# Zero matmuls between the first attention pairs: their number, their place and the PSUM bank they write

## The chip, the cores and the metric

The kernel runs on one core of a Trainium2 chip. The metric is the device time of one execution in microseconds (us), as the median of several runs. The engines are PE (matmul; PEld is its weight load), DVE (vector), ACT (scalar), POOL (gpsimd, which here mostly starts transfers) and SP (transfers). Each engine takes its own instructions in the order in which the program gives them, and waits on semaphores for the others.

## The reference

There are 8 batches, 8 heads, 576 positions and head size 64. Each head computes two attentions and adds them: one over q, k and v averaged over groups of 4 positions (144 positions, result repeated 4 times), one over a band of 7 neighbouring positions. The result goes through a gated feed-forward layer with 512 inputs and 1536 hidden units.

```
q_d = q.reshape(B, H, S/4, 4, D).mean(axis=3)        # k_d, v_d alike
out_up = repeat(softmax(scale * q_d @ k_d.T) @ v_d, 4, axis=2)
mask = abs(i - j) < 4
out_local = softmax(where(mask, scale * q @ k.T, -1e9)) @ v
x = (out_up + out_local).transpose(0, 2, 1, 3).reshape(B * S, 512)
out = (maximum(x @ w_gate, 0) * (x @ w_val)) @ w_out
```

## The kernel before

The 64 heads are worked in 32 pairs. The feed-forward layer runs over 9 chunks of 512 tokens. All orders are written out by hand: the string FRONT (L18) lists the steps of the fill, in which pairs 0 to 7 and the first chunk are brought up; ORDER (L109) is the steady state, which interleaves attention for later pairs with matmuls of the chunk that is ready; TAIL (L74) is the end. A step is a token, kind/pair/arguments, and a program loop issues the tokens one by one, so a token's place fixes its place on every engine that it uses.

The steps of the fill that matter here, for a pair p:

- loadq, loadk, loadv start the transfers of q, k and v on POOL's queue (L304, L334); only pair 0's q comes by SP's queue (L304). wg and wv fetch a quarter each of the two weight matrices (L799).
- tr/p/i/bank (emit_flip, L364) transposes q and k: 8 matmuls with 120 columns each, against an identity with pooling columns. ev copies the result from PSUM, on ACT where its token has an A, on DVE where it has a V (L378); its argument says which third, and whether the full or the pooled part.
- vd (L408) pools v with 6 matmuls into bank 6, columns 0 to 255, and vc (L417, ACT) copies that out.
- s1 (L427, L438) computes both score matrices into banks 0 to 3. ed (L462) and ex (L448) take the exponentials on ACT, and ma (L454, DVE) applies the band mask.
- sd (L475) and su (L487) multiply by v. sd writes bank 6, su banks 4 and 5. rd, td, ru, tu (L499, L504, L512, L518, all DVE) divide by the denominators and write the tile xo.
- xp (L622, L624) transposes and adds the two results on PE; xe (L634) copies them to xT, the input of the feed-forward layer.
- hv and hg (L639) are the first matmuls of the feed-forward layer.

The step warm (emit_warm, L810 to L818) issues matmuls whose two operands are the tile zero_sb, which holds zeros, and whose result nobody reads. The call before FRONT issues 12 of 128x512 into bank 7. In FRONT, warm/2 stands twice: behind pair 0's transposes and pooled v, and ahead of pair 1's pooled v (vd/1). These write 248 columns of bank 6 (264 to 511), so each is ordered against other users of that bank. In the profile all of them have line L812.

The eight PSUM banks are one tile, ps. A matmul that writes a bank waits for earlier readers of that bank where the program finds an overlap.

Of the kernel before, what the change touches and what calls it, by code (L numbers as in the profile page):

```python
# [16 lines left out]

FRONT = """  # L18
pads loadk/0 loadv/0 loadq/1 loadk/1 loadv/1 loadq/2 cast tr/0/2/4 loadk/2 ev/0/20V/4 tr/0/1/3
tr/0/0/2 ev/0/21V/4 ev/0/10A/3 vd/0/6 loadv/2 ev/0/11A/3 ev/0/01A/2 ev/0/00A/2 loadq/3 warm/2  # L20
tr/1/0/7 vc/0/6 s1/0/2 ev/1/00A/7 loadk/3 tr/1/2/1 ed/0/2 tr/1/1/0 ev/1/20V/1 ev/1/11A/0 loadv/3
sd/0/6 ev/1/21V/1 ev/1/10A/0 rd/0/6 ex/0/0/2 td/0/6 wg/0 warm/2 vd/1/6 ev/1/01A/7 ma/0/0
ex/0/1/2 s1/1/0 wv/0 ma/0/1 ed/1/0 ones/4 su/0/4 ex/1/1/0 ru/0/4 loadq/4 ex/1/0/0 tu/0/0/4
tr/2/1/2 tr/2/2/3 tu/0/1/4 ev/2/11A/2 tr/2/0/0 ev/2/10A/2 loadk/4 ev/2/21V/3 xp/0/0/4 ev/2/20V/3
ev/2/01A/0 xp/0/1/5 ev/2/00A/0 ma/1/0 loadv/4 vc/1/6 s1/2/0 ma/1/1 xe/0/0A/4 xe/0/1V/5 sd/1/6
ex/2/1/0 ones/5 su/1/4 rd/1/6 td/1/6 ed/2/0 ru/1/4 vd/2/6 loadq/5 tu/1/1/4 ex/2/0/0 tr/3/1/2
tu/1/0/4 tr/3/2/3 loadk/5 vc/2/6 tr/3/0/0 ev/3/20V/3 ev/3/10A/2 xp/1/1/5 sd/2/6 ev/3/21V/3
loadv/5 ev/3/01A/0 xe/1/1V/5 xp/1/0/4 ev/3/00A/0 ma/2/0 ev/3/11A/2 ma/2/1 xe/1/0A/4 s1/3/0 wg/1
rd/2/6 su/2/4 td/2/6 ed/3/0 ru/2/4 ex/3/0/0 tu/2/1/4 hv/0/0/7 wv/1 hv/0/1/7 tu/2/0/4 ex/3/1/0
vd/3/6 ma/3/0 ones/6 xp/2/1/5 vc/3/6 xp/2/0/4 ma/3/1 sd/3/6 xe/2/1V/5 xe/2/0A/4 loadq/6 tr/4/0/0  # L30
rd/3/6 su/3/4 td/3/6 tr/4/1/2 loadk/6 ru/3/4 hv/1/0/1 ev/4/11A/2 tu/3/0/4 hg/0/0/6 ev/4/10A/2
hg/0/1/6 tu/3/1/4 loadv/6 tr/4/2/3 ev/4/01A/0 ev/4/00A/0 xp/3/1/5 ev/4/21V/3 ev/4/20V/3 xp/3/0/4
wg/2 hv/0/2/7 xe/3/1V/5 xe/3/0A/4 hg/1/0/0 s1/4/2 wv/2 hv/0/3/7 ex/4/0/2 hv/1/1/1 loadq/7
# [136 lines left out]
def kernel(  # L170
# [50 lines left out]
    def ring(n, shape, dtype, name):  # L221
        return [keep.tile(shape, dtype, name=f"{name}{i}") for i in range(n)]
# [14 lines left out]
    ed = ring(2, [72, 2, 2 * SD + 64], FP16, "ed_")  # L237
    vd = ring(3, [72, 2, 192], FP16, "vd_")
# [11 lines left out]
    ps = psum.tile([128, 8, 512], FP32, name="ps")  # L250
# [45 lines left out]
    def emit_load_q1(hp, i):  # L296

        b, off = head_off(hp)
        src, dst, hh = (q, k)[i // 2], qk16[hp % NL][:, i // 2, :], i % 2
        if hp < NTP:  # L300
            if hh:
                return
            first = hp == 0 and src is q
            (nc.sync if first else nc.gpsimd).dma_start(  # L304
                (q32 if first else dst).rearrange("p (n d) -> p n d", d=64),
                _dap(src, off, [[D, 96], [NQ * D, 2 * NB], [1, D]]),
            )
            return
        nc.gpsimd.dma_start(  # L309
            dst.rearrange("p (j h d) -> p j h d", h=2, d=64)[:, :, hh, :],  # L310
            _dap(src, off + hh * S * D, [[D, 96], [NQ * D, NB], [1, D]]),
        )
# [182 lines left out]
    rd = ring(2, [72, 2, 2], FP32, "rd_")  # L495
    ru = ring(2, [96, 2, NB], FP32, "ru_")
# [310 lines left out]
            _dap(moe_w_out, 384 * i * D_MODEL, [[D_MODEL, 128], [128 * D_MODEL, 3], [1, D_MODEL]]),  # L807
        )

    def emit_warm(n, wide=False):  # L810
        for _ in range(n):
            nc.tensor.matmul(  # L812
                out=ps[:, 7, :] if wide else ps[:, 6, 264:512],
                lhsT=zero_sb[:, 0:128],
                rhs=zero_sb[:, 128 : 640 if wide else 376],
                start=True,
                stop=True,
            )  # L818
# [114 lines left out]
    def emit_tail_step(kind, arg, at):  # L933
        c, j = (int(at[0]), int(at[1])) if len(at) == 2 else (int(at or 0), 0)
        i = int(arg[0]) if arg else 0
        if kind in ("hg", "hv"):
            w = int(kind == "hv")
            bank = 4 + i if w else 2 * (j % 2) + i
            emit_h_mm(c, j + NK * i, w, range(4), ps[:, bank, :])
        elif kind == "relu":  # L940
            emit_relu(2 * j + i, ps[:, 2 * (j % 2) + i, :])
        elif kind == "gate":
            emit_gate(c, j + NK * i, 2 * j + i, ps[:, 4 + i, :])
        elif kind in ("gateg", "gateb"):
            nc.vector.scalar_tensor_tensor(
                out=gT[c % 2][:, j + NK * i, :],
                in0=block(c, j, 0).t[i],
                scalar=0.0,
                in1=ps[:, 4 + i, :] if kind == "gateg" else block(c, j, 1).t[i],
                op0=ALU.max,  # L950
                op1=ALU.mult,
            )
        elif kind == "xs":
            emit_xs(c, i)
        elif kind == "wg":
            emit_ws(0, i, 0, 768, nc.vector)
        elif kind == "wv":
            emit_ws(1, i, 192 * int(arg[1]), 192 * int(arg[1]) + 192, nc.gpsimd)
        elif kind in ("qg", "qv"):
            block(c, j, int(kind == "qv")).q(i)  # L960
        elif kind in ("keepg", "keepv"):
            block(c, j, int(kind == "keepv")).keep(i - 1)
        elif kind in ("tg", "tv"):
            block(c, j, int(kind == "tv")).out(arg)
        elif kind == "part":
            lo, hi = ((0, 3), (3, 5), (5, 6))[int(arg[1])]
            unit(c, j).sums(lo, hi, (i,))
        else:
            UNIT_STEPS[kind](unit(c, j), i)

    def emit_step(kind, arg, u, c):

        banks = (u, 1 - u)
        i = int(arg[-1]) if arg and arg[-1].isdigit() else 0
        if kind in H_STEPS:
            pp, jj = banks[i % 2], 6 * u + i
            if kind == "relu":
                emit_relu(i, pair(pp)[:, 0, :])
            elif kind == "gate":
                emit_gate(c, jj, i, pair(pp)[:, 1, :])  # L980
            else:
                w = int(kind == "hv")
                emit_h_mm(c, jj, w, range(4), pair(pp)[:, w, :])
        elif kind in UNIT_STEPS:
            UNIT_STEPS[kind](unit(c - 1, u), i)
        elif kind == "next":
            w = unit(c - 1, 1) if u == 0 else unit(c, 0)
            w.sums(0, NK if u == 0 else 5, (i,))
        else:
            PAIR_STEPS[kind](4 * c + 2 * u + LEAD + "ab".index(arg[0]), arg[1:])  # L990
# [45 lines left out]
    def emit_periods(c0, c1):  # L1036
        for base in range(c0, c1 + 2):
            for tok in ORDER.split():
                c = base + {">": 1, "<": -1}.get(tok[-1], 0)
                kind, arg, u = tok.rstrip("<>").split("/")  # L1040
                if c == c1 - 1 and base > c:
                    continue
                if c0 <= c < c1 or c == c0 - 1 and f"{kind}/{arg}/{u}" in LATE:
                    emit_step(kind, arg, int(u), c)

    def emit_front(tok):
        kind, *a = tok.split("/")
        if "@" in tok:
            emit_step(kind, a[0], *map(int, a[1].split("@")))
        else:  # L1050
            FRONT_STEPS[kind](*[int(x) if x.isdigit() else x for x in a])

    FRONT_STEPS = {
        "pads": emit_pads,
        "cast": lambda: nc.scalar.copy(out=qk16[0][:, 0, :], in_=q32),
        "warm": emit_warm,
        "loadq": lambda p: emit_load_q1(p, 0),
        "loadk": lambda p: emit_load_q1(p, 2),
# [37 lines left out]
    with tc.manual_schedule(engines={ET.PE, ET.DVE, ET.Activation, ET.SP, ET.Pool}):  # L1096
        nc.scalar.dma_start(cst_sb[:, 960:1080], cst_dr[:, 960:1080])
        emit_load_q1(0, 0)
        nc.sync.dma_start(cst_sb[:, 0:960], cst_dr[:, 0:960])
        nc.sync.dma_start(cst_sb[:, 1080:1368], cst_dr[:, 1080:1368])  # L1100
        emit_warm(12, True)
        for tok in FRONT.split():
            emit_front(tok)
        emit_periods(PS // 4, (NP - LEAD) // 4)
        for tok in TAIL.split():
            kind, arg, *at = tok.split("/")
            if at:
                emit_tail_step(kind, arg, at[0])
            else:
                emit_step(kind, arg, 1, NCH - 3)  # L1110
# [30 lines left out]
```

## Time and profile before

| what | value |
|---|---|
| median of 5 runs | 346.59 us |
| the 5 runs | 345.2, 345.95, 346.59, 346.63, 347.26 us |
| the profiled execution | 347.82 us |
| its span, first to last instruction | 346.0 us |
| mean granted clock of the PE | 0.984 |
| PE busy | 338.3 us, 98% |
| DVE, ACT, POOL busy | 296.0 us, 218.3 us, 182.1 us |

All times below are from the start of the span of that one profiled execution. A busy share counts an instruction from its start to its modelled end, and matmuls overlap, so a stretch with PE 100% busy need not be a full one. The granted clock is the share of full speed that the PE was given in a stretch; the record begins only at the first change, so it says 1.00 at the start of the span, whatever was granted there.

### The profile page before, as it was taken

How to read it: one execution, taken by the hardware profiler on the slowest of the kernel's cores; microseconds unless marked ns; L12 is line 12 of the kernel's file. 1: busy time of each engine (PE TensorE's matmuls, PEld its weight loads, DVE VectorE, ACT ScalarE, POOL GpSimd, SP SyncE). 2: the span in 40 equal slices, each digit the busy share in tenths (PEclk: the TensorE clock that was granted, in tenths of full speed). 3: DMA queues.
4: the chain of work that ended last, by engine and by line, in shares of the span. 5: the costliest groups of instructions: out<-in, count | busy, mean ns of one | idle time of the engine just before them, and what ended most of it. 6: DMA issues, size and time to landing. Idle time of an engine off the chain costs nothing.

```text
span 346.0 us, 8224 instructions
## 1 busy us (share of the span) xinstructions
PE 338.3 (98%) x3210; PEld 217.5 (63%) x3210; DVE 296.0 (86%) x546; ACT 218.3 (63%) x423; POOL 182.1 (53%) x232
## 2 busy tenths in 40 slices
PE   8799999999999999999999999999999999999996
PEld 3675555766565656665566657665766557768685
DVE  5676569999899999999999999999999798786892
ACT  3767876777766776677677766776677634344222
POOL 8986558685999793989287688850300000000000
PEclk9869999999999999999999999999999999999999
DMA  9999999999999999899969999993000001001023
GB/s 151 166 170 187 185 189 162 140 175 154 167 162 167 131 185 113 107 150 167 126 78 133 137 158 88 150 148 78 30 32 33 30 0 47 32 31 52 32 71 108
DMA packets 167974, 40.02 MB, mean 116 GB/s; under 512 B 149856, under 2 KB 164864, under 8 KB 167936
## 3 DMA queue, kind: packets, MB, share of 16 engines
q0 software_dynamic: 132160, 22.63, 96.0%
q1 hardware_dynamic: 35632, 16.84, 28.1%
q8 instruction: 25, 0.41, 0.5%
q14 instruction: 13, 0.11, 0.1%
q10 hardware_dynamic: 144, 0.03, 0.1%
HBM read 45.86 MB, written 9.44 MB: 160 GB/s over the span
## 4 chain that ended last, share of the span: by engine, by line
PE 94%; DMA 2%; DVE 1%; ACT 1%; issue 1%; POOL 1%; DVEq 0%; ACTq 0%; POOLq 0%
PE ps L639 50%; PE ps L724 23%; PE ps L905 4%; PE ps L585 4%; PE ps L438 3%; PE ps L427 2%; PE ps L364 2%; PE ps L593 2%; DMA qk<-in_q_dram 2%; PE ps L408 1%; PE ps L622 1%; PE ps L475 0%; DMA out_dram<-y_sb 0%; PE ps L549 0%; PE ps L624 0%
## 5 line engine op out<-in xcount | busy, mean ns | idle before, releaser
L639 PE MATMUL ps<-xT,wv_sb 128*128 128x512 f16 x432 | 109.3, 380 | 0.0
L639 PE MATMUL ps<-xT,wg_sb 128*128 128x512 f16 x352 | 88.4, 380 | 0.0
L648 ACT ACTIVATE r<-ps 128x512 f16<-128x512 f32 x88 | 52.0, 596 | 31.3 <-PE ps L639 29.2
L639 PEld LDWEIGHTS <-wv_sb 128*128 128x128 f16 x432 | 40.5, 98 | 39.7 <-issue 0.2
L651 DVE TENSOR_TENSOR gT<-r,ps 128x512 f16<-128x512 f16 x88 | 58.8, 680 | 7.3 <-PE ps L639 4.6
L639 PEld LDWEIGHTS <-wg_sb 128*128 128x128 f16 x352 | 32.6, 98 | 32.3 <-issue 0.2
L612 DVE TENSOR_TENSOR xn<-ps,rden 64x720 f16<-64x720 f32 x48 | 43.4, 905 | 4.4 <-ACT rden L608 3.0
L603 ACT ACTIVATE rden<-ps 64x720 f32<-64x720 f32 x48 | 36.7, 765 | 14.5 <-PE ps L593 13.5
L448 ACT ACTIVATE ee<-ps 112x576 f16<-112x576 f32 x64 | 38.8, 648 | 6.6 <-PE ps L438 5.6
L309 POOL DMA_DIRECT2D qk<-in_q_dram x46 | 33.7, 737 | 11.0 <-DMA vw<-in_v_dram 3.7
L309 POOL DMA_DIRECT2D qk<-in_k_dram x46 | 33.8, 737 | 8.6 <-DMA v<-in_v_dram 2.8
L724 PEld LDWEIGHTS <-gT 128*128 128x128 f16 x324 | 31.5, 98 | 9.0
L454 DVE TENSOR_TENSOR ee<-ee,cst_sb 112x576 f16<-112x576 f16 x64 | 32.0, 519 | 5.5 <-ACT ee L448 4.9
L724 PEld LDWEIGHTS <-xo 128*128 128x128 f16 x288 | 27.4, 98 | 7.4
L334 POOL DMA_DIRECT2D vw<-in_v_dram x30 | 28.5, 952 | 6.1 <-PE ps L639 2.5
L351 DVE TENSOR_REDUCE qkd<-qkT 128x288 f16<-128x1152 f16 x23 | 30.9, 1343 | 0.0
L758 ACT COPY q<-ps 128x256 f32<-128x256 f32 x45 | 16.8, 373 | 21.1 <-PE ps L724 20.8
L386 POOL TENSOR_TENSOR v<-v 72x512 f32<-72x512 f16 x21 | 25.5, 1215 | 4.8 <-DMA v<-in_v_dram 4.2
L724 PE MATMUL ps<-wo_sb,gT 128*128 128x256 f16 x216 | 28.0, 273 | 0.0
L724 PE MATMUL ps<-wt,xo 128*128 128x256 f16 x216 | 27.7, 272 | 0.0
L915 ACT COPY vw<-ps 128x256 f32<-128x256 f32 x30 | 10.8, 374 | 20.7 <-PE ps L905 13.8
L571 DVE TENSOR_TENSOR xT<-xn 128x576 f16<-128x576 f16 x28 | 22.9, 820 | 0.5
(108 smaller groups left out, 560.4 us busy)
## 6 DMA issues: line engine op xcount, KB each, us to landing
out_dram<-y_sb SPq DMA_DIRECT2D x24, 256.0 KB, 3.5
vw<-in_v_dram POOLq DMA_DIRECT2D x30, 168.0 KB, 7.3
qk<-in_q_dram POOLq DMA_DIRECT2D x46, 72.0 KB, 7.1
qk<-in_k_dram POOLq DMA_DIRECT2D x46, 72.0 KB, 7.0
v<-in_v_dram POOLq DMA_DIRECT2D x21, 144.0 KB, 7.2
out_dram<-y_sb SPq DMA_DIRECT2D x22, 128.0 KB, 1.7
wg_sb<-in_moe_w_gate_dram POOLq DMA_DIRECT2D x4, 384.0 KB, 9.9
wv_sb<-in_moe_w_val_dram POOLq DMA_DIRECT2D x4, 384.0 KB, 10.6
```

The lines of the kernel that those rows point to most:

```text
L309: nc.gpsimd.dma_start(dst.rearrange("p (j h d) -> p j h d", h=2, d=64)[:, :, hh, :], _dap(src, off + hh * S * D, [[D, 96], [NQ * D, NB], [ ...
L334: nc.gpsimd.dma_start(t, _dap(v, base, [[D, WK], [NQ * D, n], [1, D]]))
L351: nc.vector.tensor_reduce(out=qkd[hp % 2].rearrange("p i t -> p (i t)"), in_=qkT[hp % 4][:, 0 : 2 * S].rearrange("p (t f) -> p t f", f=4), ...
L386: nc.gpsimd.tensor_tensor(out=m, in0=t[:, :, 0:128], in1=t[:, :, 128:256], op=ALU.add)
L448: nc.scalar.activation(out=o, in_=ps[0:WK, p0 + 2 * g : p0 + 2 * g + 2, 0:288], func=AF.Exp, scale=scale)
L454: nc.vector.tensor_tensor(out=o, in0=o, in1=_sap(masks_sb, (0, WK), 288 * g, [[0, 2], [1, 288]]), op=ALU.mult,)
L603: nc.scalar.activation(out=rden[lo : lo + 64], in_=ps[de : de + 64, 4 + 2 * hh : 6 + 2 * hh, 0:360], func=AF.Ln)
L612: nc.vector.tensor_tensor(out=xn[lo : lo + 64], in0=ps[lo : lo + 64, 4 + 2 * hh : 6 + 2 * hh, 0:360], in1=rden[lo : lo + 64], op=ALU.mult,)
L639: nc.tensor.matmul(out=out, lhsT=w[:, kk, bass.ts(jj, 128)], rhs=xT[:, kk, c * TCH : (c + 1) * TCH], start=(kk == 0), stop=(kk == 3),)
L648: nc.scalar.activation(out=r1[j % 3], in_=h1, func=AF.Relu)
L651: nc.vector.tensor_tensor(out=gT[c % 2][:, jj, :], in0=r1[j % 3], in1=h2, op=ALU.mult)
L724: nc.tensor.matmul(out=out, lhsT=left[:, i, :], rhs=right[i], start=(first and i == 0), stop=(i == NK - 1), skip_group_check=True,)
```

## The change

The change touches the PE's order alone. DVE, ACT, POOL and SP have the same instructions in the same order before and after.

- The call ahead of FRONT issues 14 wide zero matmuls where it issued 12.
- emit_warm takes the bank as an argument, with 7 as its default; the 248-column form wrote bank 6.
- The first warm in FRONT has 5 matmuls where it had 2, still in bank 6.
- The second, 2 matmuls in bank 6 ahead of vd/1, becomes 5 in bank 7 behind vd/1 and behind the copy ev/1/01A, which reads bank 7.
- Four new groups: 5 in bank 7 between su/0 and tr/2; 1 in bank 7 between xp/0 and s1/2; 3 in bank 7 between su/1 and vd/2; 4 in bank 1 between vd/3 and xp/2.

In the program this makes 21 matmuls more on PE, 2 of 128x512 and 19 of 128x248, each with its weight load. The new waits: the first matmul of the group behind vd/1 waits for ACT (ev/1/01A has read bank 7), and the first of the group in bank 1 waits for ACT (pair 3's exponentials have read bank 1). vd/1 now itself carries the wait for td/0 on DVE, which reads bank 6; before, the zero matmul ahead of it carried it.

```diff
--- before.py
+++ after.py
@@ -17,17 +17,17 @@
-tr/0/0/2 ev/0/21V/4 ev/0/10A/3 vd/0/6 loadv/2 ev/0/11A/3 ev/0/01A/2 ev/0/00A/2 loadq/3 warm/2
+tr/0/0/2 ev/0/21V/4 ev/0/10A/3 vd/0/6 loadv/2 ev/0/11A/3 ev/0/01A/2 ev/0/00A/2 loadq/3 warm/5/6
 tr/1/0/7 vc/0/6 s1/0/2 ev/1/00A/7 loadk/3 tr/1/2/1 ed/0/2 tr/1/1/0 ev/1/20V/1 ev/1/11A/0 loadv/3
-sd/0/6 ev/1/21V/1 ev/1/10A/0 rd/0/6 ex/0/0/2 td/0/6 wg/0 warm/2 vd/1/6 ev/1/01A/7 ma/0/0
+sd/0/6 ev/1/21V/1 ev/1/10A/0 rd/0/6 ex/0/0/2 td/0/6 wg/0 vd/1/6 ev/1/01A/7 warm/5/7 ma/0/0
 ex/0/1/2 s1/1/0 wv/0 ma/0/1 ed/1/0 ones/4 su/0/4 ex/1/1/0 ru/0/4 loadq/4 ex/1/0/0 tu/0/0/4
-tr/2/1/2 tr/2/2/3 tu/0/1/4 ev/2/11A/2 tr/2/0/0 ev/2/10A/2 loadk/4 ev/2/21V/3 xp/0/0/4 ev/2/20V/3
-ev/2/01A/0 xp/0/1/5 ev/2/00A/0 ma/1/0 loadv/4 vc/1/6 s1/2/0 ma/1/1 xe/0/0A/4 xe/0/1V/5 sd/1/6
-ex/2/1/0 ones/5 su/1/4 rd/1/6 td/1/6 ed/2/0 ru/1/4 vd/2/6 loadq/5 tu/1/1/4 ex/2/0/0 tr/3/1/2
+warm/5/7 tr/2/1/2 tr/2/2/3 tu/0/1/4 ev/2/11A/2 tr/2/0/0 ev/2/10A/2 loadk/4 ev/2/21V/3 xp/0/0/4 ev/2/20V/3
+ev/2/01A/0 xp/0/1/5 ev/2/00A/0 ma/1/0 loadv/4 vc/1/6 warm/1/7 s1/2/0 ma/1/1 xe/0/0A/4 xe/0/1V/5 sd/1/6
+ex/2/1/0 ones/5 su/1/4 rd/1/6 td/1/6 ed/2/0 ru/1/4 warm/3/7 vd/2/6 loadq/5 tu/1/1/4 ex/2/0/0 tr/3/1/2
 tu/1/0/4 tr/3/2/3 loadk/5 vc/2/6 tr/3/0/0 ev/3/20V/3 ev/3/10A/2 xp/1/1/5 sd/2/6 ev/3/21V/3
 loadv/5 ev/3/01A/0 xe/1/1V/5 xp/1/0/4 ev/3/00A/0 ma/2/0 ev/3/11A/2 ma/2/1 xe/1/0A/4 s1/3/0 wg/1
 rd/2/6 su/2/4 td/2/6 ed/3/0 ru/2/4 ex/3/0/0 tu/2/1/4 hv/0/0/7 wv/1 hv/0/1/7 tu/2/0/4 ex/3/1/0
-vd/3/6 ma/3/0 ones/6 xp/2/1/5 vc/3/6 xp/2/0/4 ma/3/1 sd/3/6 xe/2/1V/5 xe/2/0A/4 loadq/6 tr/4/0/0
+vd/3/6 ma/3/0 ones/6 warm/4/1 xp/2/1/5 vc/3/6 xp/2/0/4 ma/3/1 sd/3/6 xe/2/1V/5 xe/2/0A/4 loadq/6 tr/4/0/0
 rd/3/6 su/3/4 td/3/6 tr/4/1/2 loadk/6 ru/3/4 hv/1/0/1 ev/4/11A/2 tu/3/0/4 hg/0/0/6 ev/4/10A/2
 hg/0/1/6 tu/3/1/4 loadv/6 tr/4/2/3 ev/4/01A/0 ev/4/00A/0 xp/3/1/5 ev/4/21V/3 ev/4/20V/3 xp/3/0/4
 wg/2 hv/0/2/7 xe/3/1V/5 xe/3/0A/4 hg/1/0/0 s1/4/2 wv/2 hv/0/3/7 ex/4/0/2 hv/1/1/1 loadq/7
@@ -807,10 +807,10 @@
             _dap(moe_w_out, 384 * i * D_MODEL, [[D_MODEL, 128], [128 * D_MODEL, 3], [1, D_MODEL]]),
         )
-    def emit_warm(n, wide=False):
+    def emit_warm(n, bank=7, wide=False):
         for _ in range(n):
             nc.tensor.matmul(
-                out=ps[:, 7, :] if wide else ps[:, 6, 264:512],
+                out=ps[:, 7, :] if wide else ps[:, bank, 264:512],
                 lhsT=zero_sb[:, 0:128],
                 rhs=zero_sb[:, 128 : 640 if wide else 376],
                 start=True,
@@ -1098,7 +1098,7 @@
         emit_load_q1(0, 0)
         nc.sync.dma_start(cst_sb[:, 0:960], cst_dr[:, 0:960])
         nc.sync.dma_start(cst_sb[:, 1080:1368], cst_dr[:, 1080:1368])
-        emit_warm(12, True)
+        emit_warm(14, wide=True)
         for tok in FRONT.split():
             emit_front(tok)
         emit_periods(PS // 4, (NP - LEAD) // 4)
```

## The prediction

> **What bounds the kernel now.** I read the page first, then the granted clock by stretches, then the PE's waits and its instructions in order of time.
>
> ```profile
> PE 338.3 (98%) x3210; PEld 217.5 (63%) x3210; DVE 296.0 (86%) x546; ACT 218.3 (63%) x423; POOL 182.1 (53%) x232
> PE   8799999999999999999999999999999999999996
> PEclk9869999999999999999999999999999999999999
> ```
>
> PE is the bound: busy 98%, never below 0.9 of a slice except at the two ends. The second and third digits of PEclk are the odd ones: 8 and 6, in a kernel whose mean is 0.984. Whatever the fill saves reaches the end, because behind it PE runs without gaps. The PE's waits of the first 60 us are all that it has in the whole span:
>
> ```profile
> PE ps L812 <- DVE zero_sb L271: 1.3, 1, 1.3
> PE ps L364 <- ACT ee L448: 0.8, 1, 0.8
> PE ps L812 <- DVE xo L504: 0.8, 1, 0.8
> PE ps L622 <- DVE xo L518: 0.5, 1, 0.5
> PE ps L364 <- DMA qk<-in_q_dram: 0.3, 1, 0.3
> PE ps L528 <- ACT qkT L378: 0.3, 1, 0.3
> PE ps L475 <- ACT ed L462: 0.2, 1, 0.2
> ```
>
> Columns: total us, times, longest. The waits sum to 4.2 us, none above 0.8 once PE has started. The clock costs more. Cut finely, it falls at 13.88 and is back at 24.12; that is 3 x 3.41 us, so I cut the fill in stretches of 3.41 us on that grid:
>
> ```profile
> core 0: us, PE busy (x) PEld busy (x) DVE busy (x) ACT busy (x) POOL busy (x), PEclk, DMA share, GB/s
> 3.64:7.05 3.41, 3.41 (x19) 1.29 (x19) 2.02 (x16) 0.83 (x1) 3.41 (x5) 1.00 2.12 180
> 7.05:10.47 3.42, 2.96 (x74) 2.28 (x71) 1.41 (x4) 2.91 (x9) 3.42 (x5) 1.00 2.43 155
> 10.47:13.88 3.41, 1.81 (x41) 1.50 (x39) 2.22 (x8) 2.64 (x7) 3.41 (x5) 1.00 2.44 155
> 13.88:17.29 3.41, 3.41 (x52) 2.79 (x52) 2.35 (x7) 2.30 (x8) 3.41 (x5) 0.50 1.86 183
> 17.29:20.71 3.42, 3.29 (x51) 2.82 (x50) 2.16 (x6) 2.52 (x5) 2.92 (x4) 0.50 1.73 183
> 20.71:24.12 3.41, 3.41 (x46) 2.67 (x47) 2.29 (x8) 2.13 (x6) 3.02 (x4) 0.50 2.43 157
> 24.12:27.53 3.41, 2.95 (x54) 2.26 (x53) 3.13 (x10) 1.60 (x5) 2.70 (x5) 1.00 1.78 185
> ```
>
> The stretch ahead of the fall has PE busy for 1.81 of 3.41 us (53%); the ones that kept the clock have 2.95 and more (86%). At half clock the same work takes nearly twice:
>
> ```profile
> 13.85 1.41 PE L364 MATMUL ps<-cst_sb,qk 96*64 96x120 f16 x24 [0.80 <-ACT ee L448]
> 15.19 0.42 PE L622 MATMUL ps<-cst_sb,xo 72*128 72x288 f16 x1
> 25.27 0.28 PE L622 MATMUL ps<-cst_sb,xo 72*128 72x288 f16 x1 [0.46 <-DVE xo L518]
> 32.01 0.82 PE L364 MATMUL ps<-cst_sb,qk 96*64 96x120 f16 x24
> ```
>
> **The change, part by part.** Unit: a 248-column zero matmul costs 0.105 us at full clock (the pair at L812 starts at 11.36, what follows it at 11.57), 0.21 at half. A 512-column one at the start costs 0.427 (12 starts from 1.26 to 5.93), which is half speed, though the record says 1.00 there.
>
> *The two at the start.* Twelve end at 6.36; tr/0 waits for k of pair 0 (issued 1.28, landed 5.2 later, 6.48) and starts at 6.52. Fourteen end, with full clock from 7.05, at about 7.13. tr/0 took 0.99 because its first 0.5 us were at half clock; at full clock it takes 0.75 (the chain has 0.75 for the 24 at 32.08), so it ends at 7.88, not 7.51. vd/0 0.35: 8.23. *The group of 5 instead of 2*: 0.52, so tr/1 starts at 8.75, where it waited for q until 8.50. Cost 0.25; the 0.27 us wait hides the rest.
>
> *vd/1 ahead of the zeros.* The wait for td/0 (L504) stays and moves to vd/1: 11.61 after the shift. vd/1 0.44, five zeros 0.52 (ACT's copy of bank 7 ends at 11.28, shifted 11.53, so the new wait is over), s1/1 at 12.57 where it was 12.00. Cost now 0.57. s1/1 sets ed/1, ex/1 on ACT, so tr/2 goes from 13.85 to 14.42. *The five behind su/0* run from 13.57 to 14.09 in the wait for ACT (L448, 0.8): hidden.
>
> So far the change costs 0.57 us. Its return can only be the clock. In 10.47 to 13.88 PE would now be busy 3.41 - 0.81 = 2.6 us, 76%, between the 53% that fell and the 86% that held. Counted in columns (work at the two halves of the array at once counted once; an estimate from the instruction shapes): the fallen stretch streamed about 3000, the one ahead of it 4800; at half clock the two that did not bring the clock back 3600 and 3450, the third, which did, 3770; the first stretch of the kernel 2870 (no rise), the second 3900 (rise). One bound between 3600 and 3770 fits all of them. With the change the stretch has 400 (sd) + 768 (vd/1) + 1240 (five zeros) + 864 (s1/1) + 780 (su/0) + 730 (three of the next five) = 4780. I take the clock as held.
>
> A rule speaks against this. The Trainium skill, "TensorE: Matmul & The Clock Gate", Part 1 on the HAM clock gate and the closing table of why this matters, lets the clock fall after one idle window of about 3.4 us, and asks for no idle gap over about 3 us. Here the longest gap before the fall was 0.8 us. By the rule there is no gap to fill and the sum is the 0.57 us alone, 348.4 for the profiled execution. The trace shows a fall after a stretch 47% idle, so I go by the trace. The window length of that page does agree with the 10.24 us.
>
> *What full clock is worth from 14.42 on*, walked with full-clock rows (tr 24: 0.75 to 0.82, xp pair 0.66, s1 0.5, sd 0.25 to 0.34, su 0.5, vd 0.44) and unchanged DVE and ACT rows:
>
> - tr/2 to 15.24, xp/0 to 15.90, one zero, s1/2 waits for ACT's copies (16.05), ends 16.6; sd/1 16.95, su/1 17.45, three zeros 17.76. DVE's td/1 ends at 17.7, so vd/2 starts at 17.76 (before: 18.54) and the zeros cost about 0.06.
> - vd/2 18.2, tr/3 19.0, xp/1 and sd/2 19.93, s1/3 waits for ACT (11A, 20.05), ends 20.6; su/2 waits for the second mask on DVE (20.9), ends 21.3 (before: 23.85).
> - hv 21.75, vd/3 22.2, four zeros 22.6 in the wait for tu/2. The new ACT wait is covered: ex/3/0 ends at about 21.75. tu/2 ends on DVE at 22.8, xp/2 starts at 22.87 (before: 25.27).
>
> Gain 2.4 us, 0.57 already taken off. ACT binds next: from 12.61 to 24.87 it has 3.3 us of idle, so with the 0.57 no more than 2.7 can come off. Transfers: POOL's queue is not touched and lands as before. wv's first quarter lands at 11.95 + 8.9 = 20.85, needed at 21.3; k of pair 4 at 22.7, needed at 24.5; k of pair 6 at 32.7, needed at 34.2; v of pair 9 at 58.2, needed at 60.8. Slack is 0.45 us at the least, so 2.4 passes and 3 would not. If that cover went, hv would wait for wv.
>
> Sum: the 1.82 us around the span stay, so 347.82 - 2.4 = 345.4. That execution lay 1.23 above the median of the five. If its fall of the clock is the usual case, the same gain off the median gives 344.2. If it lay high because its clock fell for longer than in others, 345.4 is right for the median too. I take 345.1.
>
> Bounds for the unknown, the clock: nothing held costs (below) 1.3 us; all held gains at most 2.7.
>
> **The rivals.**
>
> *The clock still falls (slower).* Place: the 0.8 us wait for td/0, which no zero matmul fills now, and the sparse s1 and sd ahead of it. If the grid of 3.41 us lies otherwise, say from 8.75 to 12.16, the stretch has 480 and 960 (tr/1) + 864 (s1/0) + 520 (sd/0) + 768 (vd/1) + 260 (one zero) = 3850 columns, hardly above the bound; by busy time it is 71%. If the bound is higher than that, the clock falls and the zeros run at 0.21 each in a stage where PE has no gap: 0.57, 0.21 for the single one, about 0.5 for the three ahead of vd/2 (0.14 us idle there). That is 1.3: 347.9. For it: the bound is known only between 53% and 86%. Against: the column count. It decides from a bound above 3850 columns.
>
> *The fall is not in most runs.* By the same count, before the change only grids with a window starting between about 9.8 and 10.9 fall, a third of them. The skill's page calls the window free-running; no run here shows that, but the five times spread over 2.06 us and the profiled one is above all. Then most runs have no fall to lose, and pay 0.2 to 0.6 for the zeros, while a few gain: about 346.3. Against: without a fall I expect 345 for the kernel before, and none of five is so low.
>
> **How the numbers follow.** Held clock: 0.50, 344.2 to 345.6, likeliest 345.1. Fall stays: 0.25, 347.9 (346.9 to 348.3). Fall rare already: 0.25, 346.3 (345.3 to 347.7). About 0.3% (1.04 us) is what a measurement of this kernel tells from none: faster is below 345.55, slower above 347.63. Faster: 0.45 + 0.05 = 0.50. Same: 0.05 + 0.05 + 0.17 = 0.27. Slower: 0.20 + 0.03 = 0.23. The range 343.8 to 347.9 leaves out half of the slower case and a little below. The likeliest case alone is 344.2 to 345.6.
>
> **What would show it.** PEclk without the 8 and 6 in the first slices, mean clock near 1; tr/2 at about 14.4 with 24 matmuls in 0.8 us; xp/2 at about 22.9; ACT nearly without idle from 13 to 22; the wait for DVE's L504 still 0.8, now at L408; no wait for wv_sb. Wrong: 0.50 anywhere behind 10 us, or L812 at 0.21 a piece.

## The result, and the profile after

| | kernel before | changed kernel |
|---|---|---|
| median, all executions compared | 347.29 us (79) | 346.56 us (44, 344.98 to 349.06) |
| ratio, 95% interval | | 0.9986 (0.9973 to 1.0000) |
| profiled execution, time and span | 347.82, 346.0 | 346.51, 344.7 |
| mean granted clock of it | 0.984 | 1.00 |

The change makes no difference that this measurement can tell. Executions more than 1.5% above the fastest, which had a lowered clock wherever the clock is on record, are left out of the ratio, so it isn't the quotient of the two medians. I had forecast 345.1 and a 50% chance of faster by over 0.3%.

From the page of the changed kernel: busy time by engine, PE and the granted clock in 40 slices, the chain that ended last.

```profile
PE 335.9 (97%) x3231; PEld 215.5 (63%) x3231; DVE 295.8 (86%) x546; ACT 218.1 (63%) x423; POOL 181.6 (53%) x232
PE   7899999989999999999999999999999999999996
PEclk9999999999999999999999999999999999999999
PE 88%; DVE 6%; DMA 2%; ACT 2%; issue 1%; DVEq 0%; ACTq 0%; POOLq 0%
```

The 8 and the 6, the fall that the kernel before shows, are gone from PEclk. PE has 21 matmuls more and is busy 2.4 us less, since the fill runs at full clock. But the PE digits now have an 8 at slice 9, 69 to 78 us, that the page of before has not. In stretches of the fill (PE, PEld, DVE, ACT, POOL busy with instruction counts, then the granted clock, DMA share, GB/s):

```profile
10.47:13.88 3.41, 2.58 (x51) 2.21 (x52) 2.10 (x7) 2.41 (x7) 3.41 (x5) 1.00 2.44 159
13.88:17.29 3.41, 3.10 (x71) 2.54 (x69) 2.99 (x9) 3.30 (x10) 3.41 (x5) 1.00 1.95 176
17.29:20.71 3.42, 3.26 (x75) 2.60 (x71) 3.34 (x10) 3.15 (x9) 2.95 (x4) 1.00 1.65 187
```

The stretch that was busy 1.81 has 2.58 (I had 2.6), the clock stays at 1.00, and ACT now has 3.30 and 3.15 of 3.41 us. The instructions that the prediction timed:

```profile
14.52 0.94 PE L364 MATMUL ps<-cst_sb,qk 96*64 96x120 f16 x24 [0.27 <-ACT ee L448]
17.94 0.49 PE L408 MATMUL ps<-vw,cst_sb 112*128 112x128 f16 x6
22.88 0.28 PE L622 MATMUL ps<-cst_sb,xo 72*128 72x288 f16 x1 [0.25 <-DVE xo L518]
```

Forecast: tr/2 14.42, vd/2 17.76, xp/2 22.87. That xp/2 agrees to 0.01 us is luck: tr/0 started at 7.01, not at 7.13 behind the zeros, since it waited 1.04 us for k of pair 0, and two more profiles of this kernel (below) have xp/2 at 23.07 and 22.33. In this one PE is 25.27 - 22.88 = 2.39 us ahead of the profile of before, and still 2.39 at its first L724 (before, then changed):

```profile
60.93 1.48 PE L724 MATMUL ps<-wo_sb,gT 128*128 128x256 f16 x12
58.54 1.49 PE L724 MATMUL ps<-wo_sb,gT 128*128 128x256 f16 x12
```

At the end only 346.0 - 344.7 = 1.3 are left. The waits of PE (total, times, longest) say where the rest went:

```profile
PE ps L812 <- DVE zero_sb L271: 1.3, 1, 1.3
PE ps L364 <- DMA qk<-in_k_dram: 1.0, 1, 1.0
PE ps L585 <- DVE ee L454: 0.9, 1, 0.9
PE ps L408 <- DVE xo L504: 0.8, 1, 0.8
PE ps L364 <- ACT ee L448: 0.3, 1, 0.3
PE ps L528 <- ACT qkT L378: 0.3, 1, 0.3
PE ps L622 <- DVE xo L518: 0.2, 1, 0.2
PE ps L724 <- DVE xo L718: 0.2, 1, 0.2
```

The wait for td/0 (L504) is 0.8 at L408, as forecast, and the one at the first transposes of pair 2 has shrunk from 0.8 to 0.3. New is 0.9 at L585, where PE waits for the band mask (L454, DVE). In order of time, first the changed kernel's three instructions around it, then the same place of the kernel before, where PE doesn't wait:

```profile
71.98 2.65 DVE L454 TENSOR_TENSOR ee<-ee,cst_sb 112x576 f16<-112x576 f16 x2
73.14 1.17 POOL L386 TENSOR_TENSOR v<-v 72x512 f32<-72x512 f16 x1
74.69 0.30 PE L585 MATMUL ps<-ee,vw 112*128 112x96 f16 x3 [0.94 <-DVE ee L454]
```

```profile
73.30 1.16 POOL L386 TENSOR_TENSOR v<-v 72x512 f32<-72x512 f16 x1
73.90 0.99 DVE L718 TENSOR_TENSOR xo<-gT 128x768 f16<-128x768 f16 x1
74.81 0.81 DVE L454 TENSOR_TENSOR ee<-ee,cst_sb 112x576 f16<-112x576 f16 x2
75.98 0.29 PE L585 MATMUL ps<-ee,vw 112*128 112x96 f16 x3
```

The two masks take 2.65 us instead of 0.81. Beside them POOL adds two halves of a later v (L386). That addition starts at nearly the same time in both traces (73.14, 73.30). In the trace of before, POOL waited 1.10 us for a transfer two instructions ahead of it, so it seems to be paced by transfers. DVE and PE come 2.4 us earlier and so put another instruction beside it. Before, it met L718 (0.99 here, 0.55 elsewhere), which nobody was waiting for.

So two questions stood. Does that clash eat the gain each time, or is it one execution's chance? And was the fallen clock of the one profile of before the usual case?

### The profile page after: what moved, and what is told of

The parts are those of the page before. It is cut to its first block, busy times and chain, and to the rows that moved or that the text cites. A ratio compares the mean times of both kernels' runs of the same rounds, so it can differ in the third digit from the quotient of the medians.

```text
span 344.7 us, 8266 instructions
## 1 busy us (share of the span) xinstructions
PE 335.9 (97%) x3231; PEld 215.5 (63%) x3231; DVE 295.8 (86%) x546; ACT 218.1 (63%) x423; POOL 181.6 (53%) x232
## 4 chain that ended last, share of the span: by engine, by line
PE 88%; DVE 6%; DMA 2%; ACT 2%; issue 1%; DVEq 0%; ACTq 0%; POOLq 0%
PE ps L639 46%; PE ps L724 22%; PE ps L905 4%; PE ps L585 3%; PE ps L438 2%; PE ps L427 2%; PE ps L364 2%; PE ps L593 2%; DMA qk<-in_k_dram 2%; PE ps L408 1%; DVE ee L454 1%; DVE xn L612 1%; DVE xo L718 1%; DVE gT L651 1%; ACT rden L603 0%
## 5 line engine op out<-in xcount | busy, mean ns | idle before, releaser
L454 DVE TENSOR_TENSOR ee<-ee,cst_sb 112x576 f16<-112x576 f16 x64 | 33.3, 540 | 5.8 <-ACT ee L448 5.2
L724 PEld LDWEIGHTS <-gT 128*128 128x128 f16 x324 | 31.5, 98 | 9.0
L724 PEld LDWEIGHTS <-xo 128*128 128x128 f16 x288 | 27.3, 98 | 7.7 <-DVE xo L718 0.3
L724 PE MATMUL ps<-wo_sb,gT 128*128 128x256 f16 x216 | 28.0, 273 | 0.0
L724 PE MATMUL ps<-wt,xo 128*128 128x256 f16 x216 | 27.7, 273 | 0.2 <-DVE xo L718 0.2
L386 POOL TENSOR_TENSOR v<-v 72x512 f32<-72x512 f16 x21 | 24.8, 1182 | 3.1 <-PE ps L593 2.4
L608 ACT ACTIVATE rden<-rden 128x720 f32<-128x720 f32 x28 | 22.5, 804 | 0.7
```

Source lines behind the costliest of these rows:

```text
L386: nc.gpsimd.tensor_tensor(out=m, in0=t[:, :, 0:128], in1=t[:, :, 128:256], op=ALU.add)
L454: nc.vector.tensor_tensor(out=o, in0=o, in1=_sap(masks_sb, (0, WK), 288 * g, [[0, 2], [1, 288]]), op=ALU.mult,)
L724: nc.tensor.matmul(out=out, lhsT=left[:, i, :], rhs=right[i], start=(first and i == 0), stop=(i == NK - 1), skip_group_check=True,)
```

## The experiments

Every execution comes with its mean granted clock. I call it *held* where that is 0.998 or more. A stretch of 3.41 us at half clock takes 0.5 x 3.41 / 346 = 0.005 from the mean, so a fall of three stretches gives 0.985 or less. (Values of 0.998 and 0.999 come from half clock in the last microsecond of the span, as in the profiles of f3 and f4.) The kernels e1 to e4 share the executions of the first series of the kernel before, f1 to f4 those of the second. The changed kernel's ratio is to the 79 executions of the section above, whose clocks are not on record.

| kernel | executions | held | median of the held, us | median of all, us | ratio to before (95%) |
|---|---|---|---|---|---|
| before, first series | 64 | 27 | 346.68 | 349.57 | |
| before, second series | 69 | 27 | 346.03 | 348.77 | |
| changed kernel | 44 | 40 | 346.51 | 346.56 | 0.9986 (0.9973 to 1.0000) |
| e1_v2_late | 12 | 10 | 346.37 | 346.36 | 0.9969 (0.9937 to 1.0002) |
| e2_v2_clash_before | 22 | 9 | 346.50 | 349.63 | 1.0007 (0.9967 to 1.0046) |
| e3_gap_filled | 20 | 18 | 346.44 | 346.55 | 0.9952 (0.9923 to 0.9982) |
| e4_gap_and_v2_late | 22 | 19 | 346.51 | 346.56 | 0.9956 (0.9928 to 0.9984) |
| f1_no_fill_zeros | 16 | 1 | 347.54 | 349.64 | 1.0054 (1.0022 to 1.0087) |
| f2_after_less_four_groups | 22 | 20 | 346.56 | 346.60 | 0.9962 (0.9934 to 0.9991) |
| f3_before_plus_four_groups | 22 | 18 | 346.12 | 346.45 | 0.9950 (0.9925 to 0.9976) |
| f4_narrow_zeros | 22 | 5 | 346.00 | 349.91 | 1.0033 (0.9995 to 1.0072) |

Two columns carry most of what follows. "Held" goes from 27 of 64 and 27 of 69 before to 40 of 44. That is not the changed kernel's series alone: e3 and e4 have 18 of 20 and 19 of 22 beside the first 27 of 64, f2 and f3 have 20 and 18 of 22 beside the second 27 of 69. The median of the held is 346.0 to 346.7 in every kernel but f1, which has one such execution, whatever zeros it issues. So a ratio below 1 can be the clock alone: the executions of the kernel before in these ratios are held in 27 of 34 and 27 of 42 only.

**1. Moving POOL's addition away from the masks (e1).** In the changed kernel the token v2/b, which is L386, moves behind v4/b.

```diff
-v2/b/0@1 relu/4/0@1 o/b00/0@1 o/b01/0@1 gate/3/0@1 o/b10/0@1 ln/b0/0@1 o/b11/0@1 vd/10/0
-pool/a/0@1 v/b/0@1 p/1/1@1 ln/b1/0@1 hg/5/0@1 v4/b/0@1 inv/b/0@1 flip/12 hv/5/0@1 qk/a0/1@1
+relu/4/0@1 o/b00/0@1 o/b01/0@1 gate/3/0@1 o/b10/0@1 ln/b0/0@1 o/b11/0@1 vd/10/0
+pool/a/0@1 v/b/0@1 p/1/1@1 ln/b1/0@1 hg/5/0@1 v4/b/0@1 v2/b/0@1 inv/b/0@1 flip/12 hv/5/0@1 qk/a0/1@1
```

> The kernel after, with POOL's pooled-v addition for pair 11 (L386) moved two transfers later in POOL's queue, so that it no longer runs beside pair 9's band masks on DVE. Theory 1 (the fill saves 2.4 us, and 1.1 us are given back where this addition holds up the mask at 72 us): the wait of L585 for L454 (0.94 us) goes, the second mask takes 0.45 and not 2.28, the span is 343.4 to 343.9, about 1 us under the kernel after. Rival (DVE is simply late there because its own work is full, whoever runs on POOL): the wait stays within 0.2 us of 0.94, or comes back at the next step of DVE, and the span stays at 344.5 to 345.

The masks at 71.5 us took 0.82 and PE did not wait there (two executions without the move, below, are free of it there too, so this one can't be credited to the move). But the clash came back one period later, with two POOL instructions beside two of DVE's, and a longer wait than before:

```profile
87.18 1.74 DVE L571 TENSOR_TENSOR xT<-xn 128x576 f16<-128x576 f16 x1
88.84 2.30 DVE L454 TENSOR_TENSOR ee<-ee,cst_sb 112x576 f16<-112x576 f16 x2
88.23 1.27 POOL L392 TENSOR_TENSOR vd<-v 72x256 f16<-72x256 f32 x1
89.58 1.25 POOL L386 TENSOR_TENSOR v<-v 72x512 f32<-72x512 f16 x1
PE ps L585 <- DVE ee L454: 1.6, 1, 1.6
```

The span is 344.9 (344.7 without the move). Here too, as in the first profile of the changed kernel, the wait stands behind masks that overlap an addition. Moving it gained nothing.

**2. Provoking the clash in the kernel before (e2).** The same token moves by one transfer instead of two, to stand behind v/b.

```diff
-v2/b/0@1 relu/4/0@1 o/b00/0@1 o/b01/0@1 gate/3/0@1 o/b10/0@1 ln/b0/0@1 o/b11/0@1 vd/10/0
-pool/a/0@1 v/b/0@1 p/1/1@1 ln/b1/0@1 hg/5/0@1 v4/b/0@1 inv/b/0@1 flip/12 hv/5/0@1 qk/a0/1@1
+relu/4/0@1 o/b00/0@1 o/b01/0@1 gate/3/0@1 o/b10/0@1 ln/b0/0@1 o/b11/0@1 vd/10/0
+pool/a/0@1 v/b/0@1 v2/b/0@1 p/1/1@1 ln/b1/0@1 hg/5/0@1 v4/b/0@1 inv/b/0@1 flip/12 hv/5/0@1 qk/a0/1@1
```

> The kernel before, with the same POOL addition moved one transfer later, so that it falls on pair 9's masks there (74.8 to 75.6 us). Theory 1: a mask takes over 1 us, PE gets a wait of L585 for L454 of 0.5 to 1.2 us that the kernel before has not, and the kernel is that much slower. Rival (only DVE's load counts): no mask over 0.6 us there, no new wait, no change of time.

A miss for its purpose: the profiled execution hit no clash at 73 us (masks 0.82), so it says nothing of the price. But its clock held throughout, with the fill of the kernel before, and its span was 343.7, below the changed kernel's 344.7. That was the first sign that an execution of the kernel before whose clock holds is as quick as one of the changed kernel.

**3. Filling the last gap (e3), and both edits (e4).** In the changed kernel the five zeros behind vd/1 go ahead of it, into bank 5, into the wait for td/0. e4 has the edit of e1 as well.

```diff
-sd/0/6 ev/1/21V/1 ev/1/10A/0 rd/0/6 ex/0/0/2 td/0/6 wg/0 vd/1/6 ev/1/01A/7 warm/5/7 ma/0/0
+sd/0/6 ev/1/21V/1 ev/1/10A/0 rd/0/6 ex/0/0/2 td/0/6 wg/0 warm/5/5 vd/1/6 ev/1/01A/7 ma/0/0
```

> The kernel after, with the five zero matmuls moved from behind vd/1 to ahead of it, in bank 5 which nobody reads there, so that they run in the 0.8 us wait for td/0 (L504). If those five lie on the path as the prediction had it (0.52 us of its 0.57): vd/1 starts at the same time, s1/1 0.52 earlier, xp/2 at 22.4 and not 22.88, and the fill's saving grows from 2.4 to 2.8 or 2.9, of which hv may give back 0.1 or 0.2 in a new wait for wv_sb. The span then is 344.2 if the clash at the mask stays as it is, and may be anything from 343.2 to 344.6 if it shifts. Rival (ACT sets the pace, the zeros are free): s1/1 earlier, xp/2 within 0.1 of 22.88.

> Both of the two runs above together: zeros ahead of vd/1 in bank 5 and the POOL addition two transfers later. If both theories hold their savings add: span about 343.0 to 343.4, 1.3 to 1.7 under the kernel after. Rival (another wait takes over): no more than 0.5 under it.

PE waits of e3:

```profile
PE ps L639 <- DMA wv_sb<-in_moe_w_val_dram: 0.8, 1, 0.8
PE ps L585 <- DVE ee L454: 0.6, 1, 0.6
PE ps L585 <- DMA vw<-in_v_dram: 0.4, 1, 0.4
PE ps L408 <- DVE xo L504: 0.3, 1, 0.3
```

The zeros do leave the path (L504 from 0.8 to 0.3). In their place come a wait of 0.8 for the first quarter of wv, at hv, 21.27 us, and other waits later. The spans of e3 and e4 are 345.3 and 343.9, their held medians the same as without the edits. A PE that is faster in the fill now runs into transfers.

**4. No zeros in the fill at all (f1).** The kernel before without its two groups.

```diff
-tr/0/0/2 ev/0/21V/4 ev/0/10A/3 vd/0/6 loadv/2 ev/0/11A/3 ev/0/01A/2 ev/0/00A/2 loadq/3 warm/2
+tr/0/0/2 ev/0/21V/4 ev/0/10A/3 vd/0/6 loadv/2 ev/0/11A/3 ev/0/01A/2 ev/0/00A/2 loadq/3
-sd/0/6 ev/1/21V/1 ev/1/10A/0 rd/0/6 ex/0/0/2 td/0/6 wg/0 warm/2 vd/1/6 ev/1/01A/7 ma/0/0
+sd/0/6 ev/1/21V/1 ev/1/10A/0 rd/0/6 ex/0/0/2 td/0/6 wg/0 vd/1/6 ev/1/01A/7 ma/0/0
```

> The kernel before without the two groups of zero matmuls in FRONT (the 12 wide ones ahead of it stay). Read is the share of executions whose mean granted clock is below 0.998. Theory C (each 3.41 us window of the clock must stream about 3700 columns through PE, wherever the window happens to start): the sparsest windows of the fill fall to 2400 columns, nine in ten executions fall, against about 45 to 60 in a hundred of the kernel before. Rival G (only the length of a gap counts; zeros at half a microsecond change no gap much): the share stays at that of the kernel before.

The clock fell in 15 of 16. Stretches on the grid of the profiled execution:

```profile
10.23:13.64 3.41, 1.86 (x47) 1.63 (x44) 2.39 (x8) 2.87 (x7) 3.41 (x6) 1.00 2.43 155
13.64:17.05 3.41, 3.41 (x56) 2.79 (x53) 2.28 (x6) 2.41 (x8) 3.41 (x5) 0.50 1.95 180
17.05:20.46 3.41, 3.28 (x50) 2.72 (x48) 2.38 (x7) 2.44 (x7) 3.18 (x4) 0.50 1.65 187
20.46:23.87 3.41, 3.41 (x46) 2.62 (x45) 2.25 (x9) 2.20 (x7) 2.59 (x4) 0.50 2.41 158
```

The count of columns (matmuls at the two halves of the array at once counted once) gives about 2830 in the first of these, then 3565, 3435 and 3780; the clock came back after the last. The bound that the prediction put between 3600 and 3770 fits a second fall.

**5. Which of the groups does it (f2, f3).** f2 is the changed kernel without its four new groups (warm/5/7, warm/1/7, warm/3/7, warm/4/1). f3 is the kernel before with these four alone, and the bank argument that they need. The lines touched, shown for f2; f3 adds what is taken out here.

```diff
-warm/5/7 tr/2/1/2 tr/2/2/3 tu/0/1/4 ev/2/11A/2 tr/2/0/0 ev/2/10A/2 loadk/4 ev/2/21V/3 xp/0/0/4 ev/2/20V/3
-ev/2/01A/0 xp/0/1/5 ev/2/00A/0 ma/1/0 loadv/4 vc/1/6 warm/1/7 s1/2/0 ma/1/1 xe/0/0A/4 xe/0/1V/5 sd/1/6
+tr/2/1/2 tr/2/2/3 tu/0/1/4 ev/2/11A/2 tr/2/0/0 ev/2/10A/2 loadk/4 ev/2/21V/3 xp/0/0/4 ev/2/20V/3
+ev/2/01A/0 xp/0/1/5 ev/2/00A/0 ma/1/0 loadv/4 vc/1/6 s1/2/0 ma/1/1 xe/0/0A/4 xe/0/1V/5 sd/1/6
... (two more lines, for warm/3/7 and warm/4/1)
```

> The kernel after without its four new groups (behind su/0, ahead of s1/2, vd/2 and xp/2); the 14 wide ones, the 5 behind pair 0's pooled v and the 5 behind vd/1 stay. Theory C: about 23 in a hundred executions below 0.998, against about 12 for the kernel after. Rival: the group behind su/0 carries the whole effect, then the share is that of the kernel before, 45 to 60. Executions with the clock held take as long as those of the kernel after, within 0.3 us.

> The kernel before with the four new groups alone. Theory C: about 20 in a hundred executions below 0.998. Rival (the early changes carry the effect): 45 to 60, as before.

Either half is enough: 20 and 18 of 22 held, and the rest of both are at 0.994 or 0.995, about one stretch at half clock. Their ratios (0.9962, 0.9950) overlap those of e3 and e4, and no variant is shown to be better than the changed kernel.

**6. What the clock counts (f4).** In the changed kernel each group of five 248-column zeros becomes 13 of 16 columns. That is meant to keep PE about as busy and the gaps short (the longest from 8 to 15 us is 0.8 us in either kernel), at a sixth of the columns.

```diff
-        for _ in range(n):
+        for _ in range(n if wide else 13 * n // 5):
-                out=ps[:, 7, :] if wide else ps[:, bank, 264:512],
+                out=ps[:, 7, :] if wide else ps[:, bank, 264:280],
-                rhs=zero_sb[:, 128 : 640 if wide else 376],
+                rhs=zero_sb[:, 128 : 640 if wide else 144],
```

> The kernel after with each five zero matmuls of 248 columns replaced by thirteen of 16 columns (about the same PE time by the rows of the 65-column matmuls, 40 ns apart, but 208 columns where there were 1240). The 14 wide ones stay. Theory C (columns streamed): the clock falls in more than half of the executions. Rival B (PE's busy time, however few columns): the share below 0.998 stays at about one in ten, as in the kernel after.

One group in the trace, and the stretch that it lies in:

```profile
12.32 0.47 PE L812 MATMUL ps<-zero_sb 128*128 128x16 f16 x13
10.47:13.88 3.41, 2.54 (x76) 2.26 (x71) 2.31 (x7) 2.64 (x7) 3.41 (x5) 1.00 2.44 159
```

PE is busy 2.54 us there against 2.58 in the changed kernel, but only 5 of 22 held against 40 of 44. (The profiled execution is one of those that held, at about 3690 columns in its sparsest stretch, by the same count.) This stretch alone doesn't settle it, for f4 is not as busy everywhere: at 11.20 to 14.61 it has 2.13, and no 3.41 us of the fill in the changed kernel's first profile have less than 2.44. A stretch of f2 does, on the grid of its own clock:

```profile
11.21:14.62 3.41, 2.20 (x47) 1.86 (x48) 2.10 (x6) 2.31 (x6) 3.41 (x6) 1.00 2.42 157
```

PE was busy 2.20 us there, with about 4100 columns, and the clock held. So a bound on busy time would have to lie below 2.20. An estimate from the traces: shift a grid of 3.41 us over f4's profile in steps of 0.05 us, and a quarter of its positions have a stretch of the fill under 2.20; but 17 of 22 executions were not held. With a bound of 3650 columns the same estimate, which takes all positions as equally likely, gives 87% for f4 and 100% for f1, 54% and 58% for the two held profiles of the kernel before, 14% for f2 and f3 and 10% for the changed kernel's first profile. Not held were 17 of 22, 15 of 16, 79 of 133, 2 and 4 of 22, and 4 of 44. Busy time as the rule falls, and gaps do, since none is longer; columns streamed stand, with a bound fitted on these same traces.

**7. Two more profiles of each kernel, unchanged (g1 to g4).** They bear on the two questions above.

> The kernel before, profiled once more. If its clock holds: xp/2 (L622) of pair 2 at about 22.4, as in the held profile with v2/b moved, and the span between 343.5 and 345.5. If the clock falls: the fall lasts 10.24 us and the span is 346 to 349. Theory 1 (a held fill saves 2 us that the mask at L454 gives back in some executions only): the wait L585 for L454 is there in some of these profiles and not in others, at places that differ. Theory 2 (it belongs to a PE that is ahead): a held profile of this kernel has the wait near 73 us each time, a fallen one never.

> As the run before this one, a second execution of the same kernel: theory 1 lets the wait at L585 differ between the two even if the clock is the same, theory 2 does not.

> The changed kernel, profiled once more. Clock held, xp/2 within 0.3 of 22.88. Theory 1: the wait of 0.9 at 74.69 for L454 is gone or elsewhere, and the span moves with the sum of such waits, 343.6 to 345.5. Theory 2: it is again at 74 to 75 us with 0.7 to 1.2 us, and the span is 344.7 within 0.3.

> As the run before this one, a second execution of the changed kernel: the same two expectations.

Clock held in all four. Spans: 344.0 and 343.9 for the kernel before, 344.0 and 343.6 for the changed one. First the kernel before (g2), cut at the old grid and then at its own, which starts where its clock first rose, at 5.93 us (7.06 in the first profile of this kernel):

```profile
10.47:13.88 3.41, 1.91 (x44) 1.60 (x41) 2.21 (x7) 2.63 (x7) 3.41 (x5) 1.00 2.43 155
13.88:17.29 3.41, 2.85 (x68) 2.43 (x68) 2.98 (x10) 3.30 (x10) 3.41 (x5) 1.00 1.86 183
9.34:12.76 3.42, 2.42 (x61) 1.89 (x56) 2.15 (x6) 2.61 (x8) 3.42 (x6) 1.00 2.43 155
12.76:16.17 3.41, 2.46 (x60) 2.13 (x58) 2.71 (x8) 3.40 (x9) 3.41 (x5) 1.00 2.22 167
```

The same sparse stretch is there, 1.91 us busy, and nothing falls: on this execution's grid it is shared by two stretches with 2.42 and 2.46 (about 3870 and 4020 columns). By this count where the grid lies decides, and it differs between executions: the first rise stood at 4.37, 5.21, 5.91, 5.93, 7.06 and 7.23 us in the six profiles of the two kernels. Its fill, 0.54 us ahead of the changed kernel's first profile:

```profile
13.98 0.94 PE L364 MATMUL ps<-cst_sb,qk 96*64 96x120 f16 x24 [0.80 <-ACT ee L448]
22.35 0.28 PE L622 MATMUL ps<-cst_sb,xo 72*128 72x288 f16 x1 [0.67 <-DVE xo L518]
```

The clash, in the kernel before (g2) and then the changed kernel (g3):

```profile
71.45 2.25 DVE L454 TENSOR_TENSOR ee<-ee,cst_sb 112x576 f16<-112x576 f16 x2
72.20 1.16 POOL L386 TENSOR_TENSOR v<-v 72x512 f32<-72x512 f16 x1
73.75 0.30 PE L585 MATMUL ps<-ee,vw 112*128 112x96 f16 x3 [0.54 <-DVE ee L454]
```

```profile
72.17 0.82 DVE L454 TENSOR_TENSOR ee<-ee,cst_sb 112x576 f16<-112x576 f16 x2
74.73 1.17 POOL L386 TENSOR_TENSOR v<-v 72x512 f32<-72x512 f16 x1
73.78 0.29 PE L585 MATMUL ps<-ee,vw 112*128 112x96 f16 x3
```

Where the addition overlaps the masks they take 2.25 and PE waits; where it starts after them they take 0.82 and PE doesn't. It happens in either kernel, in some executions: g1 has the wait at 89.88 us instead (0.69), g3 and g4 list none at L585. So, as far as six profiles show, the clash is one execution's chance and does not come with the change; that the landing of the transfers sets it is the likely reason, not a tested one. The second question, how usual the fall is, two profiles can't answer; the held column does: 79 of 133 executions of the kernel before were not held.

## Why the prediction was wrong, step by step

*The zeros' own cost* (0.57 by tr/2): of the right size. tr/2 starts at 13.57 and 13.98 in the two held profiles of the kernel before, at 14.52, 14.71 and 13.97 in the three of the changed one; the means are 0.62 apart, though single executions differ by as much. Behind it the new groups are free: from tr/2 to xp/2 it is 8.37 us in both profiles before, 8.36 in all three after.

*The clock in the changed kernel* (held): right, in 40 of 44. The Trainium skill, "TensorE: Matmul & The Clock Gate", Part 1 and closing table, wants an idle window for a fall and no idle gap over about 3 us. That rule was rightly set aside: f1 fell with waits of 0.8 us at the most, and 17 of 22 executions of f4, whose profile has no longer wait there, were not held. Its free-running window agrees with the first rises above, which spread over 2.86 us.

*The walk with full-clock rows*: right. From tr/2 to xp/2 the forecast has 8.45 us and the profiles 8.36. In the profile of before it was 11.42, so the fall costs 3.05 us there.

*The base of the sum*: this is the step that failed. The 2.4 us came off 347.82, an execution whose clock had fallen, and off a median taken to be of its like. But the median of the five, 346.59 (their clocks are not on record), is what the kernel before takes with its clock held: 345.7 in two profiles, medians of 346.68 and 346.03. Such executions have no 2.4 us to give: their span is 343.9 to 344.0, the changed kernel's 343.6 to 344.7, and its held median is 346.51. The argument that I used against this, that a held kernel before would show 345 and none of five did, took the fall as the only thing that moves the time. With the clock held the kernel before still runs from 344.5 to 348.1.

*The rival "The fall is not in most runs"* gave 346.3, near the measured 346.56, but its reason was wrong. It put the fall in a third of the executions, and 79 of 133 were not held. It missed a second sparse place: in the profile of before, the 3.41 us from 8.06 on have about 3110 columns by the same count. What it had right is that the median compared lies among executions which, by their times, have no fall to lose.

*"Whatever the fill saves reaches the end"*: failed too, as far as one fallen profile shows. The fall costs 3.05 us at xp/2, but that profile's span is only 2.0 to 2.1 above the held ones. The changed kernel, about 0.6 behind at tr/2, isn't visibly behind at the end. PE does wait between 60 and 340 us, by 0.2 to 1.6 at L585 alone.

*Transfers with 0.45 of slack at hv*: too narrow to count on. PE waited for wv there in five profiles: 0.8 in e3, 0.4 in e4 and f3, 0.3 in e2 and g1. e2 came only at 21.0 and still waited until 21.29, so the landing itself, forecast for 20.85, moves.

*"The clock still falls (slower)"*, the other rival: not seen in the length that it priced. 4 of 44 executions are at 0.995, what one stretch at half clock takes from the mean, not three; their median is 348.12. Where they lost it is open.

What the change does is to take the falls from the executions of the kernel before. The profiled fall was a short one: 9 of the 133 executions are at 0.984 or 0.985, as it was, and 66 at 0.980 or below, which by the estimate above is four to eight stretches. The gain shows in the medians of all executions: in the first series 349.57 before, 346.55 and 346.56 in e3 and e4; in the second 348.77 before, 346.60 and 346.45 in f2 and f3. For the changed kernel itself they are 347.29 and 346.56. None of the longer falls was profiled.

## To carry to other kernels

One profile is one draw. Before a loss seen in it is counted as a gain, ask in how many executions it is there, and whether the median that it is taken from is of executions that have it; the granted clock listed beside each execution's time answers both. Where many engines run at over 85%, a gain of 2 us at the start of a span need not be 2 us at its end: price the first stages that will be met at another moment against transfers and POOL. Dummy matmuls that are to hold the clock should be wide, and judged by the poorest position of the grid, not by the one in the trace.

## What the runs showed of the hardware

- The clock fell after a window of 3.41 us in which PE streamed fewer than some 3600 to 3700 columns, and returned after one with more. Windows with 2830, 3030, 3420, 3435, 3545 and 3565 went with a fall or no return, 3690, 3780, 3790 and all above with a held clock or a return. Busy time does not say it: a window busy 3.41 us at half clock (f1, 13.64 to 17.05, 3565 columns) did not bring the clock back, and one busy 2.20 us (f2, about 4100 columns) held it. That zeros as operands count is shown by f3 against the kernel before: four groups of zeros, and 18 of 22 held where 27 of 69 did.
- A mask of 112x576 on DVE takes 0.45 us alone. Beside one POOL addition of 1.17 us at 72 us it took 1.4 and 1.8 us longer (g2, and the first profile of the changed kernel). The Trainium skill ("GPSIMD Engine Reference", 1. Specifications) names contention with DVE instructions that have two SBUF inputs, without a figure. The six profiles of the two kernels have 11 to 14 instructions each, masks and the additions of L571, that take over 0.15 us longer than their median, 5 to 7 us in sum, and mostly PE doesn't wait for them. Such an addition is neither needed nor enough: of these 74, 20 have none beside them, and 25 of the other 484 have one beside them for over 0.1 us (in g2 two masks at 213.99 and 215.07, 0.46 and 0.45 us long). What else it takes, and why the stretching can exceed the addition's own length, is not explained.
- Open: the executions at 0.994 or 0.995, e4's three among them. In e4's profile, which held, no 3.41 us of the fill have fewer than about 4600 columns. None of those executions was profiled.
